# Earlier key preparation for the second batch and out-of-place value splitting for the first, in a fused top-k attention and two-layer feed-forward kernel

## The chip, the cores and the metric

One core of a Trainium2 chip runs the whole kernel. The metric is device time in microseconds (us) of one execution, the median of several executions. Engines are named as in the profile: PE is TensorE (PEld its weight loads), DVE is VectorE, ACT is ScalarE, POOL is GpSimd, and SP is SyncE, whose queue issues every DMA of this kernel. All engines take their instructions in one fixed order each, and wait for one another by semaphores.

## What is computed

Attention keeps only the 32 largest scores of a row. Its output goes through a feed-forward layer with a leaky ReLU and through a second one with the Mish function:

```python
batch, n_heads, seq, head_dim = (2, 8, 576, 64)      # q, k, v, float32
scores = q @ k.T / 8
kth = the 32nd largest of each row                    # 576 scores in a row
attn = softmax(where(scores >= kth, scores, -1e9)) @ v
x = attn, heads side by side                          # 1152 tokens x 512
h = x @ w_in;  x = max(0.01 * h, h) @ w_out           # 512 -> 2048 -> 512
h = x @ w_in2; out = (h * tanh(softplus(h))) @ w_out2
```

Float32 precision is kept by writing each operand as a sum of two float16 numbers (a high and a low half), scaled by a power of two that comes from the operand's sum of squares.

## The kernel before

The 1152 tokens make nine tiles of 128, and each tile has eight heads, so there are 72 slots, slot i being tile i // 8 and head i % 8. Tiles 0 to 3 lie in the first batch, tile 4 (slots 32 to 39) has 64 tokens of each batch, and tiles 5 to 8 lie in the second. So the keys and values of the second batch are first read in slots 32 and 33 (its head pair 0), 34 and 35 (pair 1), 36 and 37 (pair 2) and 38 and 39 (pair 3).

The main loop runs over i from -2 to 71. In turn i it writes the scores of slot i + 2 (`front`: PE matmuls `sps`, two ACT copies into `sc`), the two halves of the top-32 search on DVE (`topk`, seven instructions over 576 columns for each slot, `top` and `wk`), the softmax of slot i (`weigh`: POOL `nb`, two ACT passes over `wk`), and the product with the values (`back`, from tile 3 on by way of ACT `warena L551`, POOL, a DMA transpose into `pts` and PE `av`). Beside these, each turn has its share of the feed-forward work: `step` does one group of `first` (48 matmuls of 128 columns, `ph`, and the activation on ACT, DVE and POOL) and one of `second` (12 matmuls of 512 columns, `y`). The first 17 turns also load, convert and split the weights.

Each piece is given a priority by `at(i, ...)`; a scheduler then lays out every engine's order from these priorities and from its own estimate of when operands and buffers come free. An instruction can so stand several slots away from where the loop wrote it. Nothing is reordered when the kernel runs.

Three helpers matter here. `prep_k(b, hp, kraw)` takes a pair of raw key tiles, squares them on ACT (`squares`, line 124), adds up over partitions on PE (`tot`), makes the scales on DVE (`pow2`), writes the high and low halves into a scratch `kn` (ACT line 346, DVE line 347), and brings these into the transposed tile `kst`; for the second batch by four DMA transposes on SP's queue (lines 350 and 352). `split_v(b, hp)` squares a pair of value tiles, scales each into a scratch on ACT (line 373), casts the high half back over the raw tile (line 375), and subtracts for the low half on POOL (line 376). `prep_q` does for a tile's queries what `prep_k` does for keys.

The scratch is what ties these together. `aside(0)` is a piece of `warena`, and `aside(1)` is the tile `qn`, of which there is one buffer; `split_v` uses both, `prep_k` uses both for the second batch, and `prep_q` uses `qn` for its own halves up to tile 4. The raw keys have one buffer as well (`krp`), and the values share the six buffers of `kvp` (tag `kv`) with some raw keys, and later with `pts`.

Four tables set where the second batch is treated: its keys are prepared in turns `K1` = (28, 30, 32, 34) and loaded `KL` = 1 turn before; values of the first batch are split in turns 18, 20, 22 and 24 (`VS`), those of the second in 30, 32, 34 and 36 (`VX`).

Of the kernel before, what the change touches and what calls it, by code (L numbers as in the profile page):

```python
# [8 lines left out]
F16 = mybir.dt.float16  # L9
BF16 = mybir.dt.bfloat16  # L10
F32 = mybir.dt.float32
U16 = mybir.dt.uint16
I32 = mybir.dt.int32
AF = mybir.ActivationFunctionType
ALU = mybir.AluOpType
# [3 lines left out]
def topk_attention_moe_moe2_kernel(  # L19
# [17 lines left out]
    nc = tc.nc  # L37
    P = 128
    B, H, S, D = q.shape
# [5 lines left out]
    NB = 5  # L45
# [11 lines left out]
    kvp = ctx.enter_context(tc.tile_pool(name="kvp", bufs=VB))  # L57
    krp = ctx.enter_context(tc.tile_pool(name="krp", bufs=1))
    ksp = ctx.enter_context(tc.tile_pool(name="ksp", bufs=6))
# [37 lines left out]
    def pow2(tot, n, kind, pool=None, out=None):  # L97

        u = sm.tile([P, n], I32, tag="p" + kind, name="u", bufs=1)
        nc.vector.tensor_scalar(out=u, in0=tot.bitcast(I32), scalar1=1, scalar2=0x3F800000,  # L100
                                op0=ALU.logical_shift_right, op1=ALU.bitwise_and)
        sc, iv = out or [pool.tile([P, n], F32, tag=kind + c, name=kind + c) for c in "si"]
        nc.vector.tensor_scalar(out=sc.bitcast(I32), in0=u, scalar1=-1, scalar2=(189 + PW) << 23, op0=ALU.mult,
                                op1=ALU.add)
        nc.vector.tensor_scalar(out=iv.bitcast(I32), in0=u, scalar1=(65 - PW) << 23, scalar2=None, op0=ALU.add)
        return sc, iv
# [5 lines left out]
    def side(late):  # L112

        return (ps_g, "g") if late else (ps_p, "p")

    def total(part, n, where=ps_p, tag="p"):

        t = where.tile([P, 512], F32, tag=tag, name="tot")
        nc.tensor.matmul(t[:, :n], lhsT=ones, rhs=part, start=True, stop=True)
        return t[:, :n]  # L120

    def squares(x, part, junk):

        nc.scalar.activation(junk, x, AF.Square, accum_out=part)
# [184 lines left out]
    kst, vst, kinv = {}, {}, {}  # L309

    def load_kv(src, pool, tag, b, hp):

        t = pool.tile([P, 2, NB, D], F32, tag=tag, name="raw" + tag)
        nc.sync.dma_start(
            out=t[:, :, 0:4, :],
            in_=src[b, 2 * hp:2 * hp + 2, 0:4 * P, :].rearrange("h (p i) d -> p h i d", i=4))
        for to, at0, n in (((0, S - P, P),) if src is k else ((0, S - SREM, SREM), (SREM, S - SREM, SREM))):
            nc.sync.dma_start(out=t[to:to + n, :, 4, :],
                              in_=src[b, 2 * hp:2 * hp + 2, at0:at0 + n, :].rearrange("h p d -> p h d"))
        return t  # L320

    def aside(h):

        if h:
            return qp.tile([P, 6 * P], F16, tag="qn", name="aside").bitcast(F32)[:, :NB * D]
        return warena[:, 4 * NCHW * CH + NB * P:4 * NCHW * CH + NB * P + NB * D]

    def kn_of(b, h):
        if b:
            return aside(h).bitcast(F16).rearrange("p (i n) -> p i n", n=P)  # L330
        return tmp.tile([P, NB, P], F16, tag="a", name="kn", bufs=AB)

    def prep_k(b, hp, kraw):
        part = sm.tile([P, 2], F32, tag="kpart", name="kpart", bufs=1)
        kn = kn_of(b, 0)
        for h in range(2):
            squares(kraw[:, h].rearrange("p i d -> p (i d)"), part[:, h:h + 1],
                    kn.rearrange("p i d -> p (i d)").bitcast(BF16)[:, :NB * D])
        where, tag = side(b > 0)
        ks, ki = pow2(total(part, 2, where, tag), 2, "k", ksp)  # L340
        kinv[b, hp] = ki
        st = ksp.tile([P, 2, S], F16, tag="kst", name="kst")
        for h in range(2):
            if h:
                kn = kn_of(b, h)
            nc.scalar.activation(kn[:, :, 0:D], kraw[:, h], AF.Identity, scale=ks[:, h:h + 1])
            nc.vector.scalar_tensor_tensor(out=kn[:, :, D:], in0=kraw[:, h], scalar=ks[:, h:h + 1],
                                           in1=kn[:, :, 0:D], op0=ALU.mult, op1=ALU.subtract)
            if 4 * b + hp >= K3:
                nc.sync.dma_start(out=st[:, h, :4 * P].rearrange("p (i q) -> p i q", q=P),  # L350
                                  in_=kn[:, 0:4, :].rearrange("p i d -> p (i d)"), transpose=True)
                nc.sync.dma_start(out=st[:, h, 4 * P:S], in_=kn[P - SREM:, 4, :], transpose=True)
                continue
            pt = where.tile([P, SP], F16, tag=tag, name="kt")
            nc.tensor.transpose(pt[:, S - P:S], kn[:, 4, :], identh)
            for i in range(4):
                nc.tensor.transpose(pt[:, i * P:(i + 1) * P], kn[:, i, :], identh)
            nc.scalar.copy(st[:, h, :], pt[:, :S])
        kst[b, hp] = st

    def split_v(b, hp):

        raw = vst[b, hp]
        part = sm.tile([P, 2], F32, tag="vpart", name="vpart", bufs=1)
        for h in range(2):
            a = aside(h)
            squares(raw[:, h].rearrange("p i d -> p (i d)"), part[:, h:h + 1], a.bitcast(BF16)[:, :NB * D])
        vs = sm.tile([P, 2], F32, tag="vs", name="vs", bufs=1)
        pow2(total(part, 2, *side(b > 0)), 2, "v", out=(vs, v_i[:, b, 2 * hp:2 * hp + 2]))
        for h in range(2):  # L370
            a = aside(h)
            r = raw[:, h].rearrange("p i d -> p (i d)")
            nc.scalar.activation(a, r, AF.Identity, scale=vs[:, h:h + 1])
            half = r.bitcast(F16).rearrange("p (c n) -> p c n", c=2)
            nc.scalar.copy(half[:, 0], a)
            nc.gpsimd.tensor_tensor(out=half[:, 1], in0=a, in1=half[:, 0], op=ALU.subtract)
        vsp[b, hp] = raw.rearrange("p h i d -> p h (i d)").bitcast(F16).rearrange("p h (c i d) -> p h c i d", c=2, d=D)

    vsp = {}
# [334 lines left out]
    qraw, kraw, xt1, xt2, between = {}, {}, {}, {}, {}  # L714
# [8 lines left out]
    def load_for(i):  # L723
        if i < NS:
            t, h = slots[i]
            if h == 0 and t == 0:
                qraw[t] = load_q(t)
            for bp in pairs(i):
                if bp[0] == 0 and bp not in kraw and bp not in kst:
                    place = (kvp, "kv") if bp in KV else (krp, "kr")  # L730
                    kraw[bp] = load_kv(k, *place, *bp)
# [64 lines left out]
    T16 = 3  # L796
    TK = 5
    VS = 18
    VX = 30
    XD = (5, 5)  # L800
    XB = (1, 0)
    TF = (99, 32)
# [16 lines left out]
    def at(i, late):  # L819
        tc.cur_priority = PR + int((i + 2 + late) * PS)  # L820
# [5 lines left out]
    def long(i, half):  # L826
        if 0 <= i < NS:
            return tiles[slots[i][0]].topk(slots[i][1], half)
        return iter(())

    K1 = (28, 30, 32, 34)
    KL = 1
    RATE = (1, 1, 2, 1)
    PF = 4
    LF = 6
# [7 lines left out]
    for i in range(-2, NS):  # L843
        at(i, 0)
        if i >= 0 and i % 2 == 0:
            load_for(i + LF)
            load_v_for(i)
        for bp in [(1, hp) for hp in range(H // 2)]:
            if i == K1[bp[1]] - KL:
                kraw[bp] = load_kv(k, krp, "kr", *bp)  # L850
            if i == K1[bp[1]]:
                prep_k(*bp, kraw.pop(bp))
        for n in range(i + 2 if i == -2 else i + PF, i + PF + 1):
            at(i, PP[n // 2] if n < 8 else 0)
            prep_for(n)
        at(i, PP[(i + 2) // 2] if i < 6 else 0)
        front(i + 2)
        at(i, 0.5)
        one, two = long(i, 1), long(i + 1, 0)
        going = True  # L860
        while going:
            going = next(one, "end") != "end"
            going = next(two, "end") != "end" or going
        if i >= 0:
            t, h = slots[i]
            if h == H - 1:
                at(i, XP)
            tiles[t].weigh(h)
            tiles[t].back(h)
            at(i, 0.5)  # L870
        if i % 2 == 0:
            for bp in ((0, (i - VS) // 2), (1, (i - VX) // 2)):
                if bp in vst and bp not in vsp:
                    split_v(*bp)
        if i >= 0 and h == H - 1:
            at(i, XP)
            xt1[t] = tiles.pop(t).end()
        w_work(i)
        at(i, LEAD)
        for n in range(RATE[min(i // 8, len(RATE) - 1)]):  # L880
            step(i)
    n = NS
# [35 lines left out]
```

## Time and profile before

| | |
|---|---|
| median of 3 runs | 740.26 us (739.39 to 741.46) |
| profiled execution, its own time | 744.42 us |
| its span | 742.6 us |
| busy share of the span | PE 86%, PEld 61%, DVE 73%, ACT 74%, POOL 62% |
| mean granted TensorE clock | 0.949 |

A span is the time from the first to the last instruction that the profiler saw; the execution's own time has 1.8 us more around it. A busy share is an average over very different stretches. Matmuls are pipelined, and their ends are modelled, so that a busy PE need not be a full one. No engine is near its whole span, so the reader has to look at stretches, and in them at who waits for whom.

### The profile page before, as it was taken

To read this page: it belongs to the slowest core of one execution; us is meant where nothing else is said; L and a number is where in the kernel's file an instruction comes from. 1 tells how busy PE (TensorE), PEld (TensorE's weight loads), DVE (VectorE), ACT (ScalarE), POOL (GpSimd) and SP (SyncE) were. 2 spreads that over 40 slices of the span, in tenths; PEclk is the share of its full clock that TensorE was granted. 3 is DMA by queue.
4 is the path that set the end of the run, shared out by engine and by line. 5 is a ranking of instruction groups with operands and counts; after the bars stand their busy time and mean duration, and the time that the engine had idled before them with its cause. 6 is when DMAs were issued, how large, how long until landed. Compare 5 with 4: busy or idle time off the path is not lost. (4 is left out here: it accounts for less than half of the span.)

```text
span 742.6 us, 16867 instructions
## 1 busy us (share of the span) xinstructions
PE 641.5 (86%) x6420; PEld 453.7 (61%) x6420; DVE 541.5 (73%) x1199; ACT 549.7 (74%) x1072; POOL 457.7 (62%) x724
## 2 busy tenths in 40 slices
PE   2478678989978988899899988898998998999996
PEld 1354345556667765666567657666766776777672
DVE  3988779977899947977865999898889788210122
ACT  5497697878687789877877977687688778553553
POOL 2959967668976854764654766467447666433230
PEclk9999898988958999999999999999999999999999
DMA  8753463342332110342344235334324324200000
GB/s 293 233 196 114 128 226 114 123 143 79 127 112 90 58 38 0 64 88 43 81 85 87 40 65 90 50 77 79 62 63 91 64 51 61 62 16 16 1 16 28
DMA packets 107217, 64.14 MB, mean 86 GB/s; under 512 B 93696, under 2 KB 97792, under 8 KB 107136
## 3 DMA queue, kind: packets, MB, share of 16 engines
q1 hardware_dynamic: 107136, 63.06, 33.0%
q8 instruction: 50, 0.82, 0.5%
q14 instruction: 31, 0.25, 0.1%
HBM read 41.16 MB, written 2.36 MB: 59 GB/s over the span
## 5 line engine op out<-in xcount | busy, mean ns | idle before, releaser
L625 PE MATMUL ph<-xt,warena 128*128 128x128 f16 x1152 | 204.5, 221 | 4.5 <-DVE u L100 3.5
L626 PE MATMUL ph<-xt,warena 128*128 128x128 f16 x1152 | 203.8, 221 | 2.0 <-DVE xt L611 2.0
L627 PE MATMUL ph<-xt,warena 128*128 128x128 f16 x1152 | 203.9, 221 | 0.0
L494 DVE MAX8 top<-wk 128x8 f32<-128x576 f32 x216 | 158.2, 750 | 1.2
L626 PEld LDWEIGHTS <-warena 128*128 128x128 f16 x1152 | 114.3, 99 | 11.3 <-issue 6.5
L625 PEld LDWEIGHTS <-warena 128*128 128x128 f16 x1152 | 114.5, 99 | 7.4 <-issue 1.9
L634 PE MATMUL y<-warena,gl 128*128 128x512 f16 x288 | 112.7, 391 | 6.9 <-POOL gl L664 2.6
L158 POOL TENSOR_TENSOR warena<-warena 128x256 int32<-128x256 int32 x128 | 105.3, 855 | 19.3 <-DVE warena L219 6.2
L627 PEld LDWEIGHTS <-warena 128*128 128x128 f16 x1152 | 114.1, 99 | 4.3 <-issue 2.6
L635 PE MATMUL y<-warena,gh 128*128 128x512 f16 x288 | 112.5, 391 | 0.0
L636 PE MATMUL y<-warena,gh 128*128 128x512 f16 x288 | 112.2, 390 | 0.0
L497 DVE MATCH_REPLACE8 wk<-top,wk 128x576 f32<-128x576 f32 x144 | 106.8, 742 | 0.0
L519 ACT ACTIVATE wk<-sc,nb,iv 128x576 f32<-128x576 f32 x72 | 62.3, 866 | 21.2 <-POOL nb L512 21.0
L494 DVE MAX8 top<-sc 128x8 f32<-128x576 f32 x72 | 53.8, 748 | 29.1 <-ACT sc L481 26.2
L479 PE MATMUL sps<-kst,qst 128*128 128x288 f16 (+1 forms) x320 | 63.8, 305 | 7.1 <-ACT sc L481 4.1
L661 DVE SCALAR_TENSOR_TENSOR mc<-mc,hs 128x512 f32<-128x512 f32 x36 | 25.3, 702 | 57.5 <-ACT mc L660 57.5
L648 POOL TENSOR_TENSOR gl<-lk,gh 128x512 f16<-128x512 f32 x36 | 43.1, 1196 | 32.9 <-ACT lk L647 32.2
L481 ACT COPY sc<-sps 128x288 f32<-128x288 f32 x144 | 53.2, 395 | 11.3 <-PE sps L479 10.9
L520 ACT ACTIVATE wk<-wk,nb 128x576 f32<-128x576 f32 x72 | 55.7, 774 | 4.8 <-POOL nb L516 3.5
L663 POOL TENSOR_SCALAR gh<-mc 128x512 f16<-128x512 f32 x32 | 20.1, 628 | 56.4 <-DVE mc L661 46.6
L497 DVE MATCH_REPLACE8 wk<-top,sc 128x576 f32<-128x576 f32 x72 | 53.4, 742 | 0.0
L263 PE MATMUL lp<-warena,diag 128*128 128x512 f32 x80 | 49.4, 703 | 3.0 <-POOL diag L258 2.2
(182 smaller groups left out, 1534.3 us busy)
## 6 DMA issues: line engine op xcount, KB each, us to landing
warena<-in_moe_w_in_dram SPq DMA_DIRECT2D x16, 1024.0 KB, 5.6
warena<-in_moe_w_out_dram SPq DMA_DIRECT2D x11, 1024.0 KB, 4.9
warena<-in_moe_w_out_dram SPq DMA_DIRECT2D x10, 512.0 KB, 3.3
out_dram<-o SPq DMA_DIRECT2D x9, 256.0 KB, 2.3
qr<-in_q_dram SPq DMA_DIRECT2D x8, 256.0 KB, 3.1
rawkv<-in_v_dram SPq DMA_DIRECT2D x8, 256.0 KB, 3.3
rawkr<-in_k_dram SPq DMA_DIRECT2D x6, 256.0 KB, 3.4
rawkv<-in_k_dram SPq DMA_DIRECT2D x2, 256.0 KB, 8.0
```

What stands on the lines that cost most here:

```text
L158: nc.gpsimd.tensor_tensor(out=o[:, a:a + PIECE], in0=o[:, a:a + PIECE], in1=x[:, a:a + PIECE], op=ALU.add)
L479: nc.tensor.matmul(sps[p0:p0 + n, :HS], lhsT=lq[:, c, p0:p0 + n], rhs=rk[:, half * HS:(half + 1) * HS], start=(c == 0), stop=(c == 1))
L494: queued(nc.vector.max(out=top[:, 8 * r:8 * r + 8], in_=src))
L497: queued(nc.vector.match_replace(out=wk, in_to_replace=top[:, 8 * r:8 * r + 8], in_values=src, imm_value=NEG))
L519: nc.scalar.activation(e, sc, AF.Prelu, bias=nb[:, 0:1], scale=iv, alpha=1e30)
L520: nc.scalar.activation(e, e, AF.Exp, bias=nb[:, 2:3], accum_out=self.sums[:, h:h + 1])
L625: nc.tensor.matmul(o, lhsT=wb, rhs=xa, start=(c == 0), stop=False)
L626: nc.tensor.matmul(o, lhsT=wa, rhs=xb, start=False, stop=False)
L627: nc.tensor.matmul(o, lhsT=wa, rhs=xa, start=False, stop=(c == KC - 1))
L634: nc.tensor.matmul(y, lhsT=gb, rhs=whi(j), start=(g == 0 and f == 0), stop=False)
L635: nc.tensor.matmul(y, lhsT=ga, rhs=wlo(j), start=False, stop=False)
L636: nc.tensor.matmul(y, lhsT=ga, rhs=whi(j), start=False, stop=(g == FG - 1 and f == 3))
```

## The change

Three things are done at once. The preparation of keys is cut in two: a new `norm_k` has the squares, the sum and the scales, and `prep_k` keeps the conversion and the transposes; each of load, `norm_k` and `prep_k` has a table of turns of its own. For pairs 0 to 3 of the second batch the load goes from turns 27, 29, 31, 33 to 22, 26, 28, 33, the squares from 28, 30, 32, 34 to 25, 27, 29, 33, and the conversion from 28, 30, 32, 34 to 25, 27, 32, 34. The values of the first batch are split out of place: a new tile of `kvp` takes the halves, the scaled values stay in the raw tile, the two casts become one over both heads, and `aside` isn't used. The second batch's values are split in turns 28, 30, 34 and 36.

```diff
+    knorm = {}
+
+    def norm_k(b, hp, kraw):
         part = sm.tile([P, 2], F32, tag="kpart", name="kpart", bufs=1)
         kn = kn_of(b, 0)
         for h in range(2):
             squares(kraw[:, h].rearrange("p i d -> p (i d)"), part[:, h:h + 1],
                     kn.rearrange("p i d -> p (i d)").bitcast(BF16)[:, :NB * D])
         where, tag = side(b > 0)
-        ks, ki = pow2(total(part, 2, where, tag), 2, "k", ksp)
-        kinv[b, hp] = ki
+        knorm[b, hp] = pow2(total(part, 2, where, tag), 2, "k", ksp)
+
+    def prep_k(b, hp, kraw):
+        if (b, hp) not in knorm:
+            norm_k(b, hp, kraw)
+        where, tag = side(b > 0)
+        ks, kinv[b, hp] = knorm.pop((b, hp))
+        kn = kn_of(b, 0)
         st = ksp.tile([P, 2, S], F16, tag="kst", name="kst")
...
+        new = None if b else kvp.tile([P, 2, NB, D], F32, tag="kv", name="halves")
         for h in range(2):
-            a = aside(h)
+            a = new[:, h].rearrange("p i d -> p (i d)") if new is not None else aside(h)
             squares(raw[:, h].rearrange("p i d -> p (i d)"), part[:, h:h + 1], a.bitcast(BF16)[:, :NB * D])
...
-        for h in range(2):
+        for h in range(2 if new is None else 0):
             a = aside(h)
...
+        if new is not None:
+            for h in range(2):
+                nc.scalar.activation(raw[:, h], raw[:, h], AF.Identity, scale=vs[:, h:h + 1])
+            flat = raw.rearrange("p h i d -> p h (i d)")
+            half = new.rearrange("p h i d -> p h (i d)").bitcast(F16).rearrange("p h (c n) -> p c h n", c=2)
+            nc.scalar.copy(half[:, 0], flat)
+            for h in range(2):
+                nc.gpsimd.tensor_tensor(out=half[:, 1, h], in0=flat[:, h], in1=half[:, 0, h], op=ALU.subtract)
+            raw = new
...
-    VX = 30
+    VX = (28, 30, 34, 36)
...
-    K1 = (28, 30, 32, 34)
-    KL = 1
+    KL = (22, 26, 28, 33)
+    KN = (25, 27, 29, 33)
+    K1 = (25, 27, 32, 34)
...
-            if i == K1[bp[1]] - KL:
+            if i == KL[bp[1]]:
                 kraw[bp] = load_kv(k, krp, "kr", *bp)
+            if i == KN[bp[1]]:
+                norm_k(*bp, kraw[bp])
             if i == K1[bp[1]]:
                 prep_k(*bp, kraw.pop(bp))
```

The scheduler lays out every engine anew from slot 18 on. In the rows below a line number of the changed kernel is higher than that of the kernel before by 8 in `prep_k`, by 18 behind `split_v` up to the end of the layers; `sc<-sps` is a score copy, `qn` and `qst` belong to the queries, `kpart` marks the squares of keys, and `vpart` those of values.

On ACT, in the kernel before, this stands between the second score copy of slot 31 and the first of slot 32 (twelve rows of the 21 in all):

```order
L124 ACTIVATE qn,qpart<-qr 128x512
L646 ACTIVATE gh<-ph,fac_1180 128x512
L647 ACTIVATE lk<-ph,fac_1180 128x512
L519 ACTIVATE wk<-sc,nb,iv 128x576
L417 ACTIVATE qn<-qr,qs 128x4x64
L551 CAST warena<-wk 128x576
L124 ACTIVATE warena,kpart<-rawkr 128x320
L520 ACTIVATE wk,sums<-wk,nb 128x576
L654 ACTIVATE hs<-ph,fac_2424 128x512
L656 ACTIVATE mc<-ph,iv_3805 128x512
L124 ACTIVATE warena,kpart<-rawkr 128x320
L440 COPY qst<-qt 128x1024
```

In the changed kernel this is all that stands on ACT at the same place, from the copies of slot 31 to those of slot 32:

```order
L499 COPY sc<-sps 128x288 x2
L538 ACTIVATE wk,sums<-wk,nb 128x576
L458 COPY qst<-qt 128x1024
L124 ACTIVATE aside,vpart<-rawkv 128x320
L569 CAST warena<-wk 128x576
L537 ACTIVATE wk<-sc,nb,iv 128x576
L538 ACTIVATE wk,sums<-wk,nb 128x576
L499 COPY sc<-sps 128x288 x2
```

The queries of tile 4 and the squares of key pair 1 have moved up, to slots 26 to 31, and 6 instructions are left where there were 21.

The second place is ACT around the score copies of slot 38, which need key pair 3. Before:

```order
L346 ACTIVATE aside<-rawkr,ks 128x5x64
L646 ACTIVATE gh<-ph,fac_1180 128x512
L647 ACTIVATE lk<-ph,fac_1180 128x512
L702 ACTIVATE o<-y,ivo 128x512
L124 ACTIVATE qn,qpart<-qr 128x512
L124 ACTIVATE warena,vpart<-rawkv 128x320
L417 ACTIVATE qn<-qr,qs 128x4x64
L481 COPY sc<-sps 128x288
L124 ACTIVATE aside,vpart<-rawkv 128x320
L646 ACTIVATE gh<-ph,fac_1180 128x512
L647 ACTIVATE lk<-ph,fac_1180 128x512
L481 COPY sc<-sps 128x288 x2
```

The same place in the changed kernel:

```order
L354 ACTIVATE aside<-rawkr,ks 128x5x64
L124 ACTIVATE qn,qpart<-qr 128x512
L676 ACTIVATE mc<-mc 128x512
L569 CAST warena<-wk 128x576
L677 ACTIVATE mc<-mc 128x512
L537 ACTIVATE wk<-sc,nb,iv 128x576
L124 ACTIVATE warena,vpart<-rawkv 128x320
L678 ACTIVATE mc<-mc 128x512
L435 ACTIVATE qn<-qr,qs 128x4x64
L499 COPY sc<-sps 128x288
L538 ACTIVATE wk,sums<-wk,nb 128x576
L499 COPY sc<-sps 128x288
```

The square of a value tile into `aside`, which stood between the two copies of slot 38, now stands behind both, and between the conversion of the keys and the first copy there are 8 instructions where there were 6.

The third place is POOL between the softmax offsets (`nb`) of slots 20 and 21, where the last weights are still being converted. Before, the offsets of slot 21 (the last row) come behind these:

```order
L516 TENSOR_SCALAR nb<-top,iv,nb 128x1
L648 TENSOR_TENSOR gl<-lk,gh 128x512
L158 TENSOR_TENSOR wraw<-wraw,warena 128x256 x2
L512 TENSOR_SCALAR nb<-top,iv 128x1
L514 TENSOR_SCALAR nb<-top,iv 128x1
L516 TENSOR_SCALAR nb<-top,iv,nb 128x1
```

In the changed kernel:

```order
L534 TENSOR_SCALAR nb<-top,iv,nb 128x1
L483 TENSOR_SCALAR iv<-ki,qi 128x2
L486 TENSOR_SCALAR iv<-iv 128x2
L278 TENSOR_TENSOR warena<-warena 128x512 x2
L666 TENSOR_TENSOR gl<-lk,gh 128x512
L278 TENSOR_TENSOR warena<-warena 128x512 x2
L666 TENSOR_TENSOR gl<-lk,gh 128x512
L158 TENSOR_TENSOR wraw<-wraw,warena 128x256 x4
L666 TENSOR_TENSOR gl<-lk,gh 128x512
L158 TENSOR_TENSOR wraw<-wraw,warena 128x256 x2
L530 TENSOR_SCALAR nb<-top,iv 128x1
L532 TENSOR_SCALAR nb<-top,iv 128x1
```

Thirteen elementwise passes of 256 or 512 columns now stand there in one run, where the order before had spread them over the gaps of slots 19 to 22.

## Rows read from the trace of the kernel before

**Rows 1.** Stretches: busy PE, PEld, DVE, ACT, POOL (instructions), granted clock, DMA share, GB/s.

```profile
234.00:412.00 178.00, 162.28 (x1793) 118.53 (x1792) 134.64 (x327) 148.48 (x324) 104.18 (x176) 0.97 0.28 60
412.00:621.00 209.00, 191.95 (x2273) 141.48 (x2271) 186.81 (x411) 163.09 (x331) 133.51 (x245) 0.97 0.36 66
621.00:742.00 121.00, 112.15 (x1217) 78.42 (x1214) 27.09 (x56) 61.88 (x103) 41.41 (x52) 0.99 0.13 28
```

**Rows 2.** Timeline of DVE: start, length, instruction, in square brackets idle before it.

```profile
255.54 0.74 DVE L494 MAX8 top<-sc 128x8 f32<-128x576 f32 x1
...
275.79 0.75 DVE L494 MAX8 top<-sc 128x8 f32<-128x576 f32 x1
...
323.16 0.74 DVE L494 MAX8 top<-sc 128x8 f32<-128x576 f32 x1
...
339.73 0.76 DVE L494 MAX8 top<-sc 128x8 f32<-128x576 f32 x1 [3.60 <-ACT sc L481]
...
359.47 0.73 DVE L494 MAX8 top<-sc 128x8 f32<-128x576 f32 x1
...
374.60 0.76 DVE L494 MAX8 top<-sc 128x8 f32<-128x576 f32 x1
...
380.37 0.74 DVE L494 MAX8 top<-sc 128x8 f32<-128x576 f32 x1
...
401.24 0.76 DVE L494 MAX8 top<-sc 128x8 f32<-128x576 f32 x1 [0.84 <-ACT sc L481]
...
412.43 0.74 DVE L494 MAX8 top<-sc 128x8 f32<-128x576 f32 x1
...
621.37 0.74 DVE L494 MAX8 top<-sc 128x8 f32<-128x576 f32 x1
```

**Rows 3.** Timeline of ACT between 322 and 403 us, the same columns.

```profile
326.89 0.63 ACT L124 ACTIVATE qn<-qr 128x512 bf16<-128x512 f32 x1 [2.72 <-issue]
...
399.20 0.47 ACT L124 ACTIVATE aside<-rawkv 128x320 bf16<-128x320 f32 x1 [2.09 <-DMA kst<-aside]
```

**Rows 4.** Timeline of SP's queue, the last transpose of key pair 0.

```profile
324.49 1.23 SPq L352 DMA_TRANSPOSE kst<-aside  x1
```

**Rows 5.** Waits of ACT between 234 and 412 us: total, times, longest.

```profile
ACT aside L124 <- DMA kst<-aside: 3.7, 2, 2.1
ACT qst L440 <- PE qt L439: 2.9, 3, 2.3
ACT qn L124 <- issue: 2.7, 1, 2.7
ACT sc L481 <- PE sps L479: 1.6, 2, 1.1
ACT warena L124 <- DVE qi L105: 1.2, 1, 1.2
```

**Rows 6.** ACT from 234 to 621 us by shape: busy, mean ns, idle before.

```profile
L658 ACT ACTIVATE mc<-mc 128x512 f32<-128x512 f32 x23 | 14.5, 631 | 0.8 <-POOL mc L657 0.8
...
L124 ACT ACTIVATE warena<-rawkr 128x320 bf16<-128x320 f32 x8 | 3.7, 463 | 0.6 <-POOL rawkv L376 0.5
L375 ACT CAST rawkv<-aside 128x320 f16<-128x320 f32 x8 | 3.6, 456 | 0.0
...
L695 ACT COPY ys<-y 128x512 f32<-128x512 f32 x6 | 3.4, 568 | 1.3 <-PE y L636 1.3
```

**Rows 7.** Timeline of PE, the end of one group of `second` and the start of `first`.

```profile
664.27 0.38 PE L636 MATMUL y<-warena,gh 128*128 128x512 f16 x1
664.48 0.22 PE L625 MATMUL ph<-xt,warena 128*128 128x128 f16 x1
664.54 0.22 PE L626 MATMUL ph<-xt,warena 128*128 128x128 f16 x1
```

**Rows 8.** Timeline of POOL: two conversions of weights, and what was spread.

```profile
240.99 2.28 POOL L278 TENSOR_TENSOR warena<-warena 128x512 f16<-128x512 f32 x2 [0.31 <-ACT warena L276]
...
254.19 2.83 POOL L158 TENSOR_TENSOR wraw<-wraw,warena 128x256 int32<-128x256 int32 x4
```

More of the change, by code (lines that the diff above doesn't have):

```diff
@@ L331, in kn_of @@
         return tmp.tile([P, NB, P], F16, tag="a", name="kn", bufs=AB)
-    def prep_k(b, hp, kraw):
+    knorm = {}
+    def norm_k(b, hp, kraw):
         part = sm.tile([P, 2], F32, tag="kpart", name="kpart", bufs=1)
@@ L870, in topk_attention_moe_moe2_kernel @@
             at(i, 0.5)
[L871 to L874, printed above, removed]
+        for bp in ((0, (i - VS) // 2), (1, VX.index(i) if i in VX else -1)):
+            if bp in vst and bp not in vsp:
+                split_v(*bp)
         if i >= 0 and h == H - 1:
```

## The prediction

> **What bounds the kernel now.** I read stretches first, because the page's busy shares mix an attention phase with a tail. From 621 us on PE is busy for 112.15 of 121 us while DVE has 27.09 [rows 1]: that is the feed-forward work left over, the order puts nothing new there, and I cost it at nothing. So the question is how fast the 72 slots go by. Their pace can be read on DVE, at the first search of each slot (`MAX8 top<-sc`). Slots 40 to 71 take 621.37 - 412.43 = 208.9 us for 31 steps, 6.7 us each [rows 2]. Before them four steps stand out: slot 23 to 24 takes 20.2 us (255.54 to 275.79), 31 to 32 takes 16.6, 35 to 36 takes 15.1 and 37 to 38 takes 20.9 [rows 2]. Over the pace that is 13.5 + 9.9 + 8.4 + 14.2 = 46 us, and in these steps DVE has no scores to search.
>
> That isn't 46 us to be had. From 234 to 412 us (slots 20 to 39) DVE idles 178 - 134.64 = 43.4 us, against 22.2 of 209 us behind it, but ACT is busy for 148.48 of 178, which leaves 29.5, and PE for 162.28 [rows 1]. In the gaps the two do feed-forward work and splits that have to be done at some time. So I count in ACT time: the stretch is ACT work plus ACT waits, and a change can take out waits, or move work to where ACT has room (163.09 busy of 209 us later on [rows 1]).
>
> **What causes the four steps.** Slot 32 needs the queries of tile 4. Their square on ACT starts at 326.89 after 2.72 us without a named releaser [rows 3]. It writes `qn`, the one buffer that is also `aside(1)`, and at 324.49 SP issued the last transpose out of that buffer, for key pair 0 [rows 4]; about 2.4 us later it is free, so this is a wait on scratch. Only then come scales, halves, PE transposes and scores, up to the search at 339.73, which waited 3.60 us for the score copy [rows 2]. Slots 36 and 38 have the same tie the other way round: a value square into `aside` waits for the key transposes out of it, 2.09 us at 399.20 [rows 3], twice in all for 3.7 us [rows 5], and score copies are queued behind it on ACT (in the order of slot 38 the second copy is). At slot 24 the queries of tile 3 stand behind value splits that hold the same `qn`.
>
> **The change part by part.** *Loads of keys, earlier:* nothing. No wait of ACT ends on a key load: before the squares of raw keys it idled 0.6 us in eight, 0.5 of it on POOL [rows 6]. The cover is whatever ACT does between load and square; without it a square could wait at most for one landing. The longer lead matters only because the one raw-key buffer then comes free earlier for the next pair. The four DMA transposes of pairs 0 and 1 now stand in SP's queue ahead of the first `pts` transposes; these are first needed in slot 24, where they have slack.
>
> *Queries and keys of pairs 0 and 1 off the path, and value squares behind the score copies:* the waits that this takes from ACT are 3.7 (`aside`), 2.7 (`qn`) and 2.9 (`qst`, which follows the query chain), **-9.3 us** [rows 5]. The 1.6 of score copies and the 1.2 behind the scales [rows 5] belong to pairs 2 and 3, which still come late: their conversions stay in turns 32 and 34, and the order keeps them just ahead of slots 36 and 38. Bounds: 0 if something else ends each wait at the same time, and -9.3 - 1.6 - 1.2 = -12.1.
>
> *ACT work moved out:* between the score copies of slots 20 and 40 ACT has 262 instructions in place of 275. Nine of the 13 are feed-forward activations that now come behind slot 40, at 631 ns [rows 6]: **-5.7 us**. The other four are the eight casts of the first batch's splits that become four of double width. One cast takes 456 ns [rows 6]; one of 640 columns isn't in the trace and lies between 456 and two of them, 912. The nearest row is a copy of 512 columns at 568 ns [rows 6]; the line through 320 and 512 columns, 0.58 ns a column, gives 640 columns 0.64 us, so 4 x (0.91 - 0.64) = **-1.1 us** (bounds -1.8 and 0).
>
> *What comes back behind slot 40:* with these nine go three groups of `first` and two of `second` on PE. Matmuls of 128 columns follow each other at 0.06 us and of 512 at 0.21 [rows 7], so 48 take 2.8 us and 12 take 2.6, in sum 3 x 2.8 + 2 x 2.6 = 13.6 us of PE. Behind slot 40 PE is busy for 191.95 of 209 us [rows 1]. If all its idle time there were usable, they cost 0; if none is, 13.6. DVE (186.81 busy) sets the pace there as much as PE does, so I take under a third, **+4 us**.
>
> *New long runs:* what left the four gaps now stands elsewhere. ACT has 24 instructions from the first score copy of slot 21 to that of 22, and 27 from slot 24 to 25. At about 0.6 us each [rows 6] that is 14.4 and 16.2 us, over the pace by 7.7 and 9.5. On POOL the softmax offsets of slot 21 stand behind 13 passes: four at 1.14 (2.28 for two), three like them, and six at 0.71 (2.83 for four) [rows 8], 12.2 us. Score tiles are three deep, so part is covered by slots already searched: 0 to +17.2 us; at slots 20 to 22 the weights were in the way before too, and I take **+4 us**.
>
> Second-batch value loads come later because the halves hold a `kv` buffer; their squares are behind slot 28 in the order, and I cost them at nothing.
>
> Sum: -9.3 - 5.7 - 1.1 + 4 + 4 = -8.1 us. The profiled execution took 744.42 us, 1.8 more than its span, and would become 736.3; it lies 4.2 us above the median of the runs, 740.26, and from there I forecast **732.2 us**.
>
> Here a rule speaks for less. The Trainium skill (Perfetto Trace Analysis, Identifying the Most-Contended Engine) has a kernel gain by work on its most-contended engine, and takes the occupancy of Scalar and Vector for a fair measure of how far they are from their limit. By the row ACT is busy for 83% of the stretch [rows 1]. By the rule only what leaves ACT for good counts, the 1.1 us of casts, which gives 739.2; I go by the waits, as 17% of the stretch is idle. No run here shows yet which holds.
>
> **The rivals.** *No change:* the gaps were full of feed-forward matmuls, and PE gets them back later at full price. For it: PE's 162.28 of 178 us; against it: weight loads cover only 118.53 [rows 1], so PE has spaces. The +4 behind slot 40 becomes 13.6, and the sum is +1.5: about 742, or 738 if only 10 come back.
>
> *Slower, by the long runs:* the slot-21 offsets wait out the 12.2 us on POOL, ACT holds its `wk` pass and all behind it for them, and slot 24 follows with its 27 instructions; nothing is covered. Then +17.2 in place of +4 gives +5.1, 745 us. It decides against the change from 12.1 us on (where the sum is 0). For it: step 23 to 24 before had such a run in front of it and paid its whole length; against it: the three-deep scores.
>
> *Much faster:* the stretch goes at DVE's later share, 134.64 x 209 / 186.81 = 150.6 us in place of 178 [rows 1], -27 us or 713. Against it: ACT alone has 148.48 less 6.8, so it would have to be busy for 94% of it.
>
> **How the numbers follow.** Less than 0.3% (2.2 us) a measurement of this kernel can't tell from no change. Forecast (721.5 to 737) 0.57; no change (738 to 742) 0.15; slower (743 to 750) 0.15; much faster (713 to 721.5) 0.13. Faster by over 0.3% holds the forecast and the last, 0.70; same 0.14; slower 0.16. The range goes to 721.5 (waits at -12.1, nothing coming back: -18.9) and up to 743, which leaves out most of the much faster and of the slower case.
>
> **What would show it.** In the changed profile the steps into slots 24 and 32 should be under 9 us, and those into 36 and 38 under 14 and 17; ACT's waits on `kst<-aside` and on `qn` without a releaser should be gone; some 3 first groups should be fewer before slot 40 and more behind it. New steps of over 12 us at slots 21 to 26 would say that the gaps only moved, and a stretch behind slot 40 longer than 214 us that the work came back dearer than I took it. If slot 32 still waits for its queries, the scratch wasn't the cause.

## Result and the profile after

The changed kernel takes 728.78 us (727.86 to 730.28, four runs) where the kernel before takes 739.84 on the same chip: ratio 0.9849, interval 0.9824 to 0.9873, 11.1 us less. I had forecast 732.2, 8.1 less. The profiled execution took 728.16 us, its span is 726.4.

The stretches of the changed kernel by the same slots as in [rows 1] (slots 20 to 39, 40 to 70, and the rest; same columns):

```profile
230.00:394.50 164.50, 151.72 (x1667) 114.43 (x1665) 133.38 (x322) 140.06 (x305) 100.82 (x173) 0.92 0.31 66
394.50:606.00 211.50, 200.05 (x2435) 149.01 (x2436) 192.85 (x414) 168.20 (x341) 137.51 (x248) 1.00 0.36 67
606.00:726.00 120.00, 110.43 (x1217) 77.84 (x1214) 27.65 (x56) 61.76 (x103) 41.65 (x51) 1.00 0.13 27
```

The first stretch lost 13.5 us, the second gained 2.5. Another 3.8 us lie ahead of slot 20, which starts at 229.85 us here and before at:

```profile
233.66 0.74 DVE L494 MAX8 top<-sc 128x8 f32<-128x576 f32 x1
```

No term of mine had these; a kernel with the order of before up to slot 55 (e10 below) starts slot 20 at 231.68, so that some 2 of the 3.8 us belong to the one execution. In the first stretch, ACT's work fell by 148.48 - 140.06 = 8.4 us and its idle time by 29.5 - 24.4 = 5.1. PE lost 126 matmuls there, and 162 more stand behind slot 40 (some records are missing from each trace).

The slot starts that answer to [rows 2], with a few more (DVE, first search of slots 20, 23, 24, 31, 32, 35, 36, 37, 38, 40 and 71):

```profile
229.85 0.74 DVE L512 MAX8 top<-sc 128x8 f32<-128x576 f32 x1
...
258.44 0.74 DVE L512 MAX8 top<-sc 128x8 f32<-128x576 f32 x1
276.59 0.76 DVE L512 MAX8 top<-sc 128x8 f32<-128x576 f32 x1 [2.99 <-ACT sc L499]
...
328.59 0.74 DVE L512 MAX8 top<-sc 128x8 f32<-128x576 f32 x1
334.45 0.74 DVE L512 MAX8 top<-sc 128x8 f32<-128x576 f32 x1
...
353.26 0.74 DVE L512 MAX8 top<-sc 128x8 f32<-128x576 f32 x1
361.05 0.74 DVE L512 MAX8 top<-sc 128x8 f32<-128x576 f32 x1
371.91 0.74 DVE L512 MAX8 top<-sc 128x8 f32<-128x576 f32 x1
382.65 0.76 DVE L512 MAX8 top<-sc 128x8 f32<-128x576 f32 x1
...
394.49 0.74 DVE L512 MAX8 top<-sc 128x8 f32<-128x576 f32 x1
...
605.93 0.74 DVE L512 MAX8 top<-sc 128x8 f32<-128x576 f32 x1
```

The steps into slots 32, 36 and 38 are 5.9, 7.8 and 10.7 us where they were 16.6, 15.1 and 20.9. The step into 24 is still 18.1 (20.2 before), and there are new long ones: 15.4 into slot 22 and 13.7 into slot 26; the one into 37 grew from 5.8 to 10.9. Slots 20 to 28 take 9.8 us more than before, slots 28 to 40 take 23.9 less. So slot 32 comes hardly sooner behind slot 20, for all that the step into it is gone: 334.45 - 229.85 = 104.6 us in place of 339.73 - 233.66 = 106.1. Nearly all of the gain between slots 20 and 40 lies in slots 32 to 40, which take 60.0 us in place of 72.7.

ACT in the changed kernel, timeline: the first value squares and the queries of tiles 3 and 4, which answer to [rows 3]:

```profile
222.81 0.45 ACT L124 ACTIVATE halves<-rawkv 128x320 bf16<-128x320 f32 x1
...
225.03 0.64 ACT L124 ACTIVATE qn<-qr 128x512 bf16<-128x512 f32 x1
...
310.60 0.63 ACT L124 ACTIVATE qn<-qr 128x512 bf16<-128x512 f32 x1 [1.42 <-DMA qr<-in_q_dram]
```

And its waits from 230 to 394.5 us, which answer to [rows 5]:

```profile
ACT warena L569 <- DMA pts<-warena: 7.3, 7, 1.9
ACT wk L537 <- POOL nb L530: 4.1, 4, 1.8
ACT pts L549 <- PE pt L548: 3.6, 2, 2.7
ACT sc L499 <- PE sps L497: 1.9, 3, 0.9
ACT qn L124 <- DMA qr<-in_q_dram: 1.4, 1, 1.4
```

The waits on `kst<-aside`, on `qst` and the one on `qn` without a releaser are gone. Three of the waits listed here stood there before too, and [rows 5] does not show them:

```profile
ACT warena L551 <- DMA pts<-warena: 6.2, 7, 1.9
...
ACT pts L531 <- PE pt L530: 1.8, 3, 1.2
...
ACT wk L519 <- POOL nb L512: 1.1, 2, 0.8
```

They grew: the wait on the softmax offsets (`nb`) from 1.1 to 4.1 us, the one on transposed weights of the softmax (`pt`) from 1.8 to 3.6, and the longest, on the transposes into `pts`, from 6.2 to 7.3.

### The profile page after: what moved, and what is told of

Read it like the earlier page. It is cut to its first block, busy times and chain, and to the rows that moved or that the text cites. A ratio compares the mean times of both kernels' runs of the same rounds, so it can differ in the third digit from the quotient of the medians.

```text
span 726.4 us, 16854 instructions
## 1 busy us (share of the span) xinstructions
PE 636.1 (88%) x6420; PEld 455.5 (63%) x6420; DVE 550.6 (76%) x1199; ACT 547.7 (75%) x1068; POOL 457.5 (63%) x724
## 4 chain that ended last, share of the span: by engine, by line
PE 34%; DVE 17%; ACT 16%; DMA 13%; POOL 13%; issue 7%; SPq 0%; POOLq 0%; ACTq 0%; DVEq 0%
DMA pts<-warena 6%; DVE top L512 6%; POOL warena L158 5%; PE ph L643 4%; PE ph L644 4%; PE ph L645 4%; DVE wk L515 4%; PE y L652 4%; PE y L654 4%; PE y L653 4%; DMA warena<-in_moe_w_in_dram 3%; PE lp L263 2%; ACT wk L537 2%; PE sps L497 2%; POOL warena L570 2%
## 5 line engine op out<-in xcount | busy, mean ns | idle before, releaser
L652 PE MATMUL y<-warena,gl 128*128 128x512 f16 x288 | 110.4, 383 | 6.9 <-ACT o L720 2.2
L654 PE MATMUL y<-warena,gh 128*128 128x512 f16 x288 | 110.2, 383 | 0.0
L653 PE MATMUL y<-warena,gh 128*128 128x512 f16 x288 | 110.0, 382 | 0.0
L530 POOL TENSOR_SCALAR nb<-top,iv 128x1 f32<-128x1 f32 x72 | 25.2, 350 | 47.0 <-DVE top L512 40.0
```

The costliest lines, as they stand in the source:

```text
L652: nc.tensor.matmul(y, lhsT=gb, rhs=whi(j), start=(g == 0 and f == 0), stop=False)
L653: nc.tensor.matmul(y, lhsT=ga, rhs=wlo(j), start=False, stop=False)
L654: nc.tensor.matmul(y, lhsT=ga, rhs=whi(j), start=False, stop=(g == FG - 1 and f == 3))
```

## The experiments

All steps and stretches below are differences between first searches of slots on DVE in each kernel's profiled run. Of each kernel: ratio to the kernel before, and the time of slots 20 to 27, 28 to 39, 40 to 70, and from slot 71 to the end of the span.

| kernel | ratio, interval | 20-28 | 28-40 | 40-71 | rest |
|---|---|---|---|---|---|
| before | 1 | 72.4 | 106.3 | 208.9 | 121.2 |
| changed | 0.985 (0.982 to 0.987) | 82.2 | 82.4 | 211.4 | 120.5 |
| e1 values only | 0.987 (0.981 to 0.993) | 80.9 | 93.8 | 201.0 | 121.0 |
| e2 keys only | 0.990 (0.987 to 0.993) | 72.5 | 108.0 | 201.7 | 119.1 |
| e3 loads only | 0.994 (0.991 to 0.997) | 71.3 | 111.0 | 200.5 | 119.1 |
| e4 queries apart | 0.994 (0.991 to 0.998) | 77.7 | 105.8 | 199.3 | 118.1 |
| e5 own scratch | 0.990 (0.986 to 0.994) | 74.1 | 97.4 | 209.1 | 121.1 |
| e6 own, head 0 | 0.996 (0.994 to 0.999) | 78.4 | 103.7 | 201.5 | 121.6 |
| e7 own, head 1 | 0.991 (0.988 to 0.995) | 70.5 | 112.7 | 200.1 | 119.1 |
| e8 old value turns | 0.988 (0.985 to 0.992) | 82.2 | 84.4 | 210.7 | 123.2 |
| e9 value turns only | 0.993 (0.990 to 0.997) | 72.8 | 109.7 | 199.0 | 121.4 |
| e10 regrouped late | 0.989 (0.983 to 0.994) | 72.6 | 106.2 | 203.6 | 116.1 |
| e11 two turns earlier | 0.985 (0.979 to 0.991) | 80.5 | 82.9 | 216.8 | 120.9 |
| e12 lead 7 | 0.985 (0.980 to 0.990) | 79.7 | 91.3 | 196.0 | 129.4 |

**The parts alone.** First the values' half of the change, with the keys loaded, squared and converted at their old turns, and the second batch's values split at theirs. This diff and the next are against the changed kernel:

```diff
-    VX = (28, 30, 34, 36)
+    VX = (30, 32, 34, 36)
...
-    KL = (22, 26, 28, 33)
-    KN = (25, 27, 29, 33)
-    K1 = (25, 27, 32, 34)
+    KL = (27, 29, 31, 33)
+    KN = (28, 30, 32, 34)
+    K1 = (28, 30, 32, 34)
```

> Only the values of the first batch are split out of place; the keys keep their old turns (loads 27, 29, 31, 33; squares and conversion 28, 30, 32, 34), and the second batch's values theirs (30, 32, 34, 36). Theory A, that the in-place split held the scratch which queries and keys wait for, expects most of the gain here: the order has 8 ACT instructions between the copies of slots 31 and 32 where the kernel before has 21, so the step into slot 32 falls from 16.6 to under 9 us, while those into 36 and 38 stay at 13 to 21; time 0.985 to 0.993 of before. Rival B, that the longer lead of the keys makes the gain, expects no change (0.997 to 1.003) and a long step into slot 32.

730.74 us. The step into slot 32 is 6.0 already; those into 36 and 38 are 13.7 and 17.5. But slots 20 to 40 take 174.7 us, only 4.0 less than before; 8.1 us of what its trace gains lie behind slot 40. Then the keys' half, with all values split in place and at their old turns, as before:

```diff
-        new = None if b else kvp.tile([P, 2, NB, D], F32, tag="kv", name="halves")
+        new = None if True else kvp.tile([P, 2, NB, D], F32, tag="kv", name="halves")
...
-    VX = (28, 30, 34, 36)
+    VX = (30, 32, 34, 36)
```

> Only the keys' three tables are new; all values are split in place, as before, in their old turns. Theory A expects the steps into slots 24 and 32 to stay at 15 us or more (the order has 36 and 35 ACT instructions ahead of them), and those into 36 and 38 to fall by 2 to 5 us each: 0.993 to 1.003 of before. Rival B expects nearly the whole gain, 0.983 to 0.990.

733.58 us. Without the values it only moves the gap: into slot 32 27.0 us in place of 16.6, into 36 6.1 in place of 15.1. Its ratio, 0.990, lies at the upper end of what rival B had for the keys alone, and outside the range of theory A; a later run (e10 below) shows that an edit which touches no wait of the sum can bring as much. The two parts alone lose 1.3 and 1.0%, together 1.5: they don't add up. The two in one kernel, without the new turns of the second batch's values (e8 below), are at 0.988, so that the keys add nothing to the values' half that these intervals could show: they take another 9.4 us out of slots 28 to 40 (93.8 to 84.4), and slots 40 to 71 get 9.7 longer (201.0 to 210.7).

**Two edits that close no gap.** The loads of keys alone, which I had priced at nothing, and the query halves of tiles 3 and 4 in buffers of another pool, which by my reading should have closed two gaps:

```diff
-    KL = 1
+    KL = (22, 28, 30, 32)
...
-            if i == K1[bp[1]] - KL:
+            if i == KL[bp[1]]:
```

> Only the loads of the second batch's keys come earlier (turns 22, 28, 30, 32; squares and conversions in their old turns). Theory A prices earlier loads at nothing: 0.997 to 1.003, no step changed by more than 2 us before slot 39. Rival B expects 0.990 or less. Rival C, that any new layout by the scheduler moves the time by a per cent or so, expects a change beyond 0.3% of either sign, with the steps changed at places that have nothing to do with keys.

```diff
-                qn = qp.tile([P, 6 * P], F16, tag="qn", name="qn")
+                if t in (3, 4):
+                    qn = ksp.tile([P, 2, S], F16, tag="kst", name="qn").rearrange("p a b -> p (a b)")[:, :6 * P]
+                else:
+                    qn = qp.tile([P, 6 * P], F16, tag="qn", name="qn")
```

> The kernel before, but the queries of tiles 3 and 4 take their halves from the pool of the transposed keys instead of the buffer that the scratch shares. If sharing that one buffer is what kept the queries back (the reading in the prediction), the steps into slots 24 and 32 fall to 9 us or less and the time to 0.985 to 0.992. If the value splits are late for another reason and the queries stand behind them in the order (24 and 43 ACT instructions are still ahead of these slots), both steps stay above 13 us, and the time within 0.4% of before.

735.06 and 736.04 us, both faster by 0.6%, though the stretch from slot 20 to 40 got longer, 182.3 and 183.5 us in place of 178.7. The queries of tile 3 come at 271.2 us (268.98 before) and those of tile 4 stayed at 326.9. That speaks less against the shared `qn` than it seems: the pool that I took the buffers from also stages raw weights, of which POOL reads the last from 269.7 us on, so one tie may have been put in place of another.

**Which scratch holds the values back.** In the kernel before, the square of head 1 runs at 176.13 us into `aside(1)`, which is `qn`; the square of head 0 goes into `aside(0)`, which is part of the words where the last weights are staged, and waits for them:

```profile
257.06 0.47 ACT L124 ACTIVATE warena<-rawkv 128x320 bf16<-128x320 f32 x1 [0.34 <-POOL wraw L158]
```

For all that time half a value pair holds the queries' buffer. Three kernels split in place as before, but give the first batch's splits a scratch of their own, for both heads, for head 0 or for head 1:

```diff
+        own = None if b else kvp.tile([P, 2, NB, D], F32, tag="kv", name="own")
...
-            a = aside(h)
+            a = aside(h) if b else own[:, h].rearrange("p i d -> p (i d)")
```

> The kernel before, whose first-batch values are still split in place, with single casts, but through a scratch tile of their own in place of aside (both heads). If it is the scratch that holds the splits back (head 0's lies where the last weights are staged, head 1's is the queries' buffer), this gives what the values' part alone gave: ratio about 0.987, some 730 to 731 us; the first value squares at about 222 us in place of 257, the queries of tile 3 behind them at about 225, the step into slot 32 under 8 us. If the gain comes from the out-of-place form (one cast for two heads, no cast over the raw tile), it stays near 0.994, where two edits that moved nothing of this also were. If any new layout gives the same, also 0.994.

> As the run with the scratch of its own, but only for head 0 (the piece that lies where the weights are staged); head 1 still uses the queries' buffer. If the staging alone was the block, the first value squares come at about 222 us, the queries of tile 3 by slot 21, and the ratio is that of both heads, 0.987. If both buffers bind, the queries of tile 4 still stand in slot 31 behind the splits and keys that hold their buffer, the step into slot 32 stays at 14 to 17 us, and the ratio is 0.990 to 0.995.

> As the run with the scratch of its own, but only for head 1 (the queries' buffer is free of value splits of the first batch); head 0 still uses the piece where the weights are staged. My reading in the prediction was that the queries' buffer held the queries of tiles 3 and 4: by it the steps into slots 24 and 32 both fall by 8 us or more, and the ratio is 0.987 or lower. If the staging is the block, the queries of tile 3 come early, at about 225 us, but the value squares of head 0 still at 257, the keys and the queries of tile 4 with them, the step into slot 32 stays at 14 to 17 us, and the ratio is 0.993 to 1.

| own scratch for | first squares, heads 0 and 1 | queries of tiles 3, 4 | steps into 24, 32 |
|---|---|---|---|
| none (before) | 257.06, 176.13 | 268.98, 326.89 | 20.2, 16.6 |
| head 0 | 224.77, 174.60 | 240.35, 324.31 | 11.2, 7.3 |
| head 1 | 255.54, 223.51 | 225.51, 322.05 | 16.8, 14.4 |
| both | 223.76, 224.21 | 225.99, 301.83 | 14.8, 5.8 |

So both pieces bind. Freeing `qn` alone brings the queries of tile 3 up by 43 us, those of tile 4 by 5: they now wait for the key transposes out of the same buffer, which in the kernel with head 1 apart the trace names (ACT timeline):

```profile
322.05 0.63 ACT L124 ACTIVATE qn<-qr 128x512 bf16<-128x512 f32 x1 [1.28 <-DMA kst<-aside]
```

Only with both free do they come 25 us earlier. A shorter step is not yet a gain: with head 0 apart the step into slot 32 is 7.3 us, where I had expected 14 to 17 if both pieces bind, but slots 20 to 32 take 106.5 us as they took 106.1 before; they take 103.9 with head 1 apart and 98.8 with both.

The times tell less than the places. The run with both apart, 734.20 us, is 1.0% faster, but an interval of 0.986 to 0.994 holds both values that I had written down, 0.987 and 0.994, and an edit of the next paragraph (e10) brings as much without freeing anything. So what the scratch alone is worth is not shown by this ratio, nor what the double-width cast and the scaling in place add to it; what is shown is that freeing both pieces brings the queries up and takes slots 20 to 40 from 178.7 to 171.5 us.

**How much any new order moves.** The changed kernel with the second batch's value turns put back (30, 32, 34, 36), and the kernel before with the new ones (28, 30, 34, 36):

> The changed kernel with the second batch's values split in turns 30, 32, 34 and 36 again. None of my terms hangs on these turns: by them the ratio is that of the changed kernel, 0.985, within 0.3%. If a new layout by itself moves the time, it comes out up to 0.6% away from that, 0.979 to 0.991, with the steps of slots 28 to 40 much the same.

> The kernel before with one line of the change, the second batch's values in turns 28, 30, 34 and 36; up to slot 32 the order is that of before, then it differs. By my terms it touches no wait of the sum: ratio 1.000, within 0.3%. If any new order behind slot 32 does what the runs with the keys' loads alone and with the queries' halves apart showed, and the order of before is a poor one there, it is 0.992 to 0.997, with the four steps of [rows 2] as they were and the time lost behind slot 32 elsewhere.

733.37 and 736.03 us. The line that I priced at nothing makes the kernel before 0.7% faster, with its slots 20 to 40 longer by 3.8 us. The sharpest of these runs asks for three feed-forward groups in other turns; its order is the one of before up to slot 55:

```diff
-        for n in range(RATE[min(i // 8, len(RATE) - 1)]):
+        for n in range(RATE[min(i // 8, len(RATE) - 1)] - (i in (23, 31, 35)) + (i in (45, 53, 61))):
```

> The kernel before with three feed-forward groups asked for in turns 45, 53 and 61 in place of 23, 31 and 35; the order comes out as that of before up to slot 55 and another from there on. By my terms 1.000, within 0.3%. If part of the gain is only that the order of before is a poor one behind slot 40 (the waits of PE for transposed weights between 412 and 518 us lie ahead of slot 56), this keeps that part and is 1.000 too; if it lies behind slot 56, it is 0.994.

732.57 us: the second ground of my expectation was right in kind, and its 0.994 is the upper end of the interval. Its stretches, columns as in [rows 1]:

```profile
231.70:410.40 178.70, 165.43 (x1801) 121.89 (x1799) 135.07 (x328) 148.86 (x325) 104.32 (x177) 0.95 0.29 60
410.40:614.00 203.60, 191.95 (x2309) 142.17 (x2307) 185.82 (x412) 165.17 (x333) 135.48 (x244) 0.98 0.37 69
614.00:730.00 116.00, 108.10 (x1178) 75.71 (x1176) 26.42 (x55) 59.45 (x100) 40.44 (x52) 0.99 0.12 27
```

Slots 20 to 40 take 178.7 us as before, with the four steps at 20.2, 15.8, 15.1 and 21.3: no gap was touched, and 1.1% is gained all the same. Where, the first searches of slots 20, 40, 56 and 71 in this kernel show, with that of slot 56 before below them:

```profile
231.68 0.74 DVE L494 MAX8 top<-sc 128x8 f32<-128x576 f32 x1
...
410.51 0.74 DVE L494 MAX8 top<-sc 128x8 f32<-128x576 f32 x1
...
512.50 0.76 DVE L494 MAX8 top<-sc 128x8 f32<-128x576 f32 x1 [2.76 <-ACT sc L481]
...
614.09 0.74 DVE L494 MAX8 top<-sc 128x8 f32<-128x576 f32 x1
```

```profile
518.00 0.76 DVE L494 MAX8 top<-sc 128x8 f32<-128x576 f32 x1 [2.78 <-ACT sc L481]
```

The two profiled executions lie 742.6 - 730.1 = 12.5 us apart. Up to slot 55 both run the same order, so the 2.0 us ahead of slot 20 and the 3.6 of slots 40 to 55 (102.0 in place of 105.6) are a difference between two executions and not the order's. The new order has the other 7.0: 1.8 us in slots 56 to 70 (101.6 in place of 103.4) and 5.2 behind slot 71. One thing that is shorter behind slot 40 is PE's waiting for transposed softmax weights. Waits of PE from slot 40 to the end, in the kernel before, in this one and in the changed one:

```profile
PE av L565 <- DMA pts<-eh: 7.8, 5, 2.3
PE av L565 <- DMA pts<-warena: 6.0, 6, 2.3
```

```profile
PE av L565 <- DMA pts<-eh: 5.7, 4, 2.3
PE av L565 <- DMA pts<-warena: 2.0, 4, 0.7
```

```profile
PE av L583 <- DMA pts<-warena: 4.9, 4, 1.4
PE av L583 <- DMA pts<-eh: 2.5, 2, 1.3
```

13.8 us became 7.7 and 7.4. Of these, what lies behind slot 56, where the orders differ, before and in this kernel:

```profile
PE av L565 <- DMA pts<-eh: 3.7, 3, 1.8
...
PE av L565 <- DMA pts<-warena: 1.6, 2, 1.4
```

```profile
PE av L565 <- DMA pts<-eh: 0.4, 1, 0.4
...
PE av L565 <- DMA pts<-warena: 0.3, 1, 0.3
```

There 5.3 us became 0.7.

**Versions of the changed kernel.** First-batch values two turns earlier, `VS = (16, 18, 20, 22)`. In this kernel slots 17, 19, 21 and 23 multiply by values that the split has already scaled, so it computes something else there; the instructions are the same in number and size. And a lead of the feed-forward of 7 turns, `LEAD = 7.0`:

> The changed kernel with the first batch's values split in turns 16, 18, 20 and 22. The order has 20, 23 and 16 ACT instructions in the runs of slots 21, 24 and 37 where the changed kernel has 24, 27 and 22. If these runs of ACT set the steps into slots 22, 24 and 38 (15.4, 18.1 and 10.7 us), each loses 0.6 us an instruction, 2.4 + 2.4 + 3.6, and the ratio is 0.976 to 0.981. If feed-forward work fills whatever they leave, so that only the idle time of PE counts, it is 0.985, within 0.4%.

> The changed kernel with a lead of the feed-forward groups of 7 turns in place of 5; the order is that of the changed kernel up to slot 25, another behind it, and the last tile keeps six instructions more for the tail. None of my terms hangs on it: 0.985, within 0.3%. If new orders alone move the time by up to 0.6%, 0.979 to 0.991.

731.06 and 730.18 us. With fewer ACT instructions in the runs ahead of slots 22, 24 and 38, the steps there are 16.0, 17.2 and 8.8 in place of 15.4, 18.1 and 10.7: the first didn't fall, the other two by less than I worked out, and in that kernel slots 40 to 71 take 5.4 us more. Neither beats the changed kernel. The longer lead, which none of my terms hangs on, left the ratio at 0.985.

## Why the number was right and part of the reason was not

**The four steps.** Right for three: into 32, 36 and 38 under 9, 14 and 17 us, as I wrote they would be. Wrong for slot 24: 18.1, not under 9. The queries of tile 3 did move up, from 268.98 to 225.03, but in front of the first score copy of slot 24 ACT still has a full run of weight conversion, value splits and feed-forward. The prediction named a sign that the gaps only moved, new steps of over 12 us at slots 21 to 26, and two came, into 22 and 26. Up to slot 32 they did only move (104.6 us in place of 106.1 from slot 20 on); from there to slot 40 they did not. The tie through `qn` that I gave as the cause is one of two: the run with head 1 apart shows that the value splits let go of it late because of their other scratch, which the prediction left out.

**ACT's waits** (-9.3 and, for the new long runs, +4). ACT's idle time in the stretch fell by 5.1 us, where these two terms give 5.3. The waits that went are the ones that I named, but the new runs cost more: slots 20 to 28 got 9.8 us longer, within my bound of 17.2, and the runs of slots 28 to 40 gave back more than I had counted.

**Work moved out** (-5.7 and -1.1): ACT's work fell by 8.4 us in place of 6.8. The 640-column cast takes 0.71 to 0.75 us in its four rows, where I had put 0.64, so that this term was about 0.7 and not 1.1.

**What comes back behind slot 40** (+4) is the term that was mis-sized, though 2.5 us between the two traces looks like a hit. The kernel before is a poor yardstick behind slot 40. In its profiled run 208.9 + 121.2 = 330.1 us pass there, 3.6 of them of that execution alone. In the four kernels that touch none of my waits in effect (e3, e4, e9, e10) it is 317.4 to 320.4, in the mean 319.3. In the six in which the first batch's values are free of both ties (the changed kernel, e1, e5, e8, e11, e12) it is 322.0 to 337.7, mean 330.2. (e2, e6 and e7, which move the keys alone or free one of the two pieces, stand in neither group; their ratios have the same mean as those of the four, 0.9926.) Against each other the six take 168.6 from slot 20 to 40 and the four 181.8. So the freed scratch, in four of the six with the new turns of the keys, takes 13.2 us out of slots 20 to 40, about the 12.1 that I had, but 10.9 come back, not 4; my full price for these groups was 13.6. (By the table, the two kernels without the keys' turns, e1 and e5, take 173.1 us there, the other four 166.4.) That is what the rival "no change" said of PE: its spaces before slot 40 were mostly full.

**What I had no term for** made up the difference: each of the four new orders was faster than the one of before, in part because that one waits for `pts` behind slot 40. So the forecast came near by luck as well, as two errors nearly cancel: 6.9 us of returned work that I left out, and the gain of a new order that I did not foresee. The ratios of the four have the mean 0.9926 (0.989 to 0.994), of the six 0.9867 (0.985 to 0.990): at 740 us that is 5.5 for the new order alone and 4.4 for the change's own mechanism, and the changed kernel lies another 1.3 below the mean of the six. Single orders differ by 0.5% within either group, so this split, which is worked out from two groups of kernels and not tried in one, is good to 2 or 3 us. Why the order of before waits more for `pts` is shown only as far as the rows go; which entries of SP's queue are to blame was not tried.

**The rival from the rule:** the Trainium skill (Perfetto Trace Analysis, Identifying the Most-Contended Engine) takes the engine with the highest occupancy as the one to optimize first. That only work taken from ACT for good counts, which gave 739.2, was my own step from there; the page does not say it. The runs do not bear this step out: with three groups asked for in other turns, ACT was busy for 148.86 + 165.17 + 59.45 = 373.48 us from slot 20 on, against 373.45 in [rows 1], and the kernel was 8 us faster.

**The other rivals:** slower by the long runs did not come, though these runs cost more than I took; the fast case (713) failed, as slots 20 to 40 took 164.5 us and not 150.6, with ACT busy for 85% of them, and as 10.9 us came back.

## What to carry to other kernels

Where a scheduler lays out the order, run two or three edits that should do nothing beside the change: here they moved the kernel before by 0.6 to 1.1%, beside the 1.5% that the change seemed to bring, and the changed kernel by 0 to 0.3%. A scratch that two pieces of work share can tie up a third: half a value split held the queries' buffer for 81 us because its other half waited for weight staging elsewhere. And work that leaves a gap should be priced at its full length where it comes back, unless the engine there is idle in kernels with another order too.

## What the runs showed of the hardware

A short wait of PE can cost more than its length. In the changed kernel PE waits twice ahead of slot 25 (PE timeline; then stretches of 4 us, columns as in [rows 1]):

```profile
276.54 1.12 PE L548 MATMUL pt<-identf,wk 128*128 128x128 f32 x4 [2.36 <-ACT sc L499]
278.60 0.59 PE L119 MATMUL tot<-kpart,one 128*128 128x2 f32 x2 [0.94 <-ACT warena L124]
...
282.10 0.31 PE L643 MATMUL ph<-xt,warena 128*128 128x128 f16 x1
282.21 0.31 PE L644 MATMUL ph<-xt,warena 128*128 128x128 f16 x1
```

```profile
270.00:274.00 4.00, 3.71 (x56) 3.32 (x54) 1.25 (x3) 4.00 (x12) 2.77 (x3) 1.00 0.00 0
274.00:278.00 4.00, 1.30 (x6) 0.72 (x4) 1.41 (x4) 4.00 (x13) 2.48 (x4) 0.66 0.31 82
278.00:282.00 4.00, 3.40 (x15) 3.08 (x16) 4.00 (x12) 3.05 (x8) 3.12 (x8) 0.50 0.36 85
282.00:286.00 4.00, 4.00 (x40) 3.91 (x39) 3.79 (x10) 3.94 (x10) 1.60 (x3) 0.56 0.17 33
286.00:290.00 4.00, 4.00 (x35) 2.53 (x33) 3.97 (x7) 3.21 (x7) 2.34 (x5) 1.00 0.23 44
```

In the stretch of the first wait PE is busy for 1.30 of 4 us and the granted clock is 0.66; behind it the clock is 0.50, the lower level of 1.2 GHz, and then 0.56, for some 8 us, and matmuls of 128 columns follow each other at 0.11 us in place of 0.06 [rows 7]. So the new gaps of slots 20 to 28 help to lower the clock of slots 20 to 40 to 0.92 (0.97 in [rows 1], but 0.95 in the kernel regrouped from slot 56 on, which has the same order there), while behind slot 40, where the returned work leaves fewer waits, it rises from 0.97 to 1.00. The profiled run of the kernel before has the same behind slot 48, where PE waits 2.28 us for a transfer of `pts`:

```profile
466.00:470.00 4.00, 1.72 (x34) 1.46 (x32) 3.93 (x10) 2.07 (x5) 2.30 (x6) 1.00 0.91 78
470.00:474.00 4.00, 4.00 (x21) 2.02 (x22) 3.97 (x11) 3.00 (x6) 1.33 (x3) 0.57 0.00 0
```

Not every such wait is followed by a lower clock. Behind the longest wait of PE in that kernel from slot 40 on the clock of the stretch is 1.00:

```profile
502.67 0.22 PE L625 MATMUL ph<-xt,warena 128*128 128x128 f16 x1 [2.79 <-DVE u L100]
```

```profile
502.00:506.00 4.00, 3.33 (x61) 3.14 (x61) 3.96 (x11) 2.83 (x7) 1.66 (x3) 1.00 0.42 78
```

In the kernel that is regrouped from slot 56 on, the same order of slots 48 to 55 has no such wait for `pts` at its start and a clock of 1.00 in its first 16 us, and takes 51.5 us in place of 55.2. These 3.7 us are about as much as the 4.2 by which the profiled execution lay above the median; how many other executions lack the wait isn't seen, since one of each kernel was profiled.
